# Closing feed-forward stage: where the cast and the lower half of a weight part stand in the engines' queues

## The chip, the cores and the metric

The kernel runs on one core of a Trainium2 chip. The metric is the device time of one execution in microseconds (us), the median of three runs. Engines: PE is TensorE (PEld its weight loads), DVE is VectorE, ACT is ScalarE, POOL is GpSimd, SP is SyncE, which issues the DMAs spoken of here.

## The reference

Three layers follow one another: an attention layer (2 batches, 8 heads, 576 positions, head width 64, rotary positions), a layer of 8 experts with top-1 routing over the 1152 tokens, and a dense feed-forward layer. Only the last one is touched:

```python
def _moe2_ref(x, w_in, w_out, alpha):      # x 1152x512, w_in 512x2048, w_out 2048x512
    h = x @ w_in
    g = np.maximum(h, 0.0) + alpha * np.minimum(h, 0.0)
    return (g @ w_out).astype(np.float32)
```

The rows of `x` that no expert kept are zero, and the kernel sorts the kept tokens into columns, so that the closing stage runs over 784 columns with these inputs.

## The kernel before, in words

Every product is made of three passes (`PASS`): each float32 operand is split into an upper half, a cast to fp32r, and a lower half, what is left; the passes are upper x upper, upper x lower, lower x upper. The weights of the closing layer come from memory as 64-bit numbers.

The closing stage is `ffn`, called by `short_way` with the blocks (272, 256, 256) and the tag "a". The hidden width of 2048 is 16 steps `f`, and four steps are a quarter `mg`. `up(f)` makes three blocks, one for each range of columns: twelve matmuls on PE into one of four PSUM banks (L1124), two Relu of that bank on ACT (L1133, L1134), a sum of them on DVE (L1136, called the blend here), a cast on ACT (L1141) and the lower half on POOL (L1142). The cast and the lower half of a block are put into the list `later` and enter the queues at the next `flush()`, which stands behind the two Relu of the next block. `down(mg)` makes six tiles of 128 columns, twelve matmuls each (L1188), summed by DVE (L1198, L1200) out of three PSUM banks in turn. Behind the first of the six tiles stands `down_strip` (L1157), eight narrow matmuls for the 16 columns left over, which need a copy by POOL (L1146) from the last block of each step `f`. The order is up(0) to up(4), down(0), up(5) to up(8), down(1), up(9) to up(12), down(2), up(13) to up(15), down(3). So three times a run of up blocks ends in a first tile.

A weight group `g` has four parts: group 2*mg is the quarter of w_in that up uses, group 2*mg+1 the quarter of w_out that down uses. `split2` turns one part (128 x 512) into its two halves: three DVE instructions at once (L1020 to L1022, bit operations that make a float32 of a 64-bit number), and `rest`, returned for later: a cast on ACT (L1025) and a subtraction on POOL (L1026, the lower half of the part). The buffer `raw2` that a group lies in is loaded again by `load2`, a DMA on SP, once its last part is split.

`pace()` is called at the end of each block and each tile and counts them in `slots[0]`: slots 1 to 15 are up blocks, 16 to 21 tiles, 22 to 33 blocks, 34 to 39 tiles, 40 to 51 blocks, 52 to 57 tiles, 58 to 66 blocks, 67 to 72 tiles. `piece()` starts one part: group 1 at the ends of slots 7, 8, 9, 10, group 4 at 14, 16, 18, 20, group 3 at 22, 24, 26, 28, group 6 at 32, 34, 36, 38, group 5 at 40, 42, 44, 46, group 7 at 48, 50, 52, 54. `need(g)` stands ahead of the first use of a group and flushes: group 1 ahead of slot 16, 4 ahead of 31, 3 ahead of 34, 6 ahead of 49, 5 ahead of 52, 7 ahead of 67.

The program order is each engine's order: the schedule is written by hand, and every engine takes its own instructions in that order.

Of the kernel before, what the change touches and what calls it, by code (L numbers as in the profile page):

```python
# [845 lines left out]
def build(nc, tc, cap, q, k, v, wg, w1, w2, w_in, w_out, alpha, tab, rtab, out):  # L846
    assert 0 < cap <= W
    with ExitStack() as top:
# [149 lines left out]
        with ExitStack() as ctx:  # L998
# [12 lines left out]
            def w2_hl(g):  # L1011
                return hl[(3, 0, 2, 1)[g % 4]]

            def split2(src, ht, c):


                hw, lw = src[:, :, 1], src[:, :, 0]
                t = cv[:, next(turns)]
                v = nc.vector
                v.tensor_scalar(t, hw, 3, 0x3FFFFFFF, op0=ALU.logical_shift_left, op1=ALU.bitwise_and)  # L1020
                v.scalar_tensor_tensor(hw, hw, 0xC0000000, t, op0=ALU.bitwise_and, op1=ALU.bitwise_or)
                v.scalar_tensor_tensor(hw, lw, 29, hw, op0=ALU.logical_shift_right, op1=ALU.bitwise_or)  # L1022

                def rest():
                    nc.scalar.copy(ht[:, 0, c], hw.bitcast(F32))  # L1025
                    nc.gpsimd.tensor_tensor(ht[:, 1, c], hw.bitcast(F32), ht[:, 0, c].bitcast(F32), op=ALU.subtract)  # L1026

                return rest

            def rows64(dst, src):  # L1030
                nc.sync.dma_start(
                    dst.rearrange("p c f w -> p c (f w)"), src.bitcast(U32).rearrange("(c p) f -> p c f", p=P)
                )
# [3 lines left out]
            def src2(c):  # L1037
                mg = c // 2
                if c % 2 == 0:
                    return w_in[:, mg * 512 : mg * 512 + 512]  # L1040
                return w_out[mg * 512 : mg * 512 + 512, :]

            def make_ffn(zp, gp, tp, pf, po, pt):
# [11 lines left out]
                def ffn(c0, blocks, tag, first, early=()):  # L1055
# [6 lines left out]
                        side = pt(f"side_{tag}")  # L1062
                        nc.vector.memset(gs, 0.0)

                    done, later = [0, 0], []

                    def flush():
                        while later:
                            later.pop(0)()

                    seq = ([0, 2] if first else []) + [1, 4, 3, 6, 5, 7]
                    raw_of = lambda g: raw2[seq.index(g) % 2]
                    src_of = lambda g, c: rawy[:, c] if g == 1 and c < 2 and not first else raw_of(g)[:, c]
                    pieces = [(g, c) for g in seq for c in range(4)]

                    def load2(i):
                        if i < len(seq):
                            g = seq[i]
                            half = g == 1 and not first
                            rows64(raw_of(g)[:, 2 if half else 0 : 4], src2(g)[256 if half else 0 : 512])  # L1080
# [5 lines left out]
                    def piece(n=1):  # L1086

                        for _ in range(n):
                            if not pieces or pieces[0][0] // 2 - 1 > done[pieces[0][0] % 2]:
                                return  # L1090
                            g, c = pieces.pop(0)
                            later.append(split2(src_of(g, c), w2_hl(g), c))
                            if c == 3 and not (strip and g % 2):
                                later.append(lambda: load2(seq.index(g) + 2))

                    slots = [0]

                    def pace():


                        slots[0] += 1
                        if (slots[0] > LEAD or first) and (slots[0] % 2 == 0 or slots[0] <= 2 * LEAD and not first):
                            piece()

                    def need(g):

                        while any(p[0] == g for p in pieces):
                            n = len(pieces)
                            piece()
                            assert len(pieces) < n  # L1110
                            flush()
                        flush()

                    def up(f):
                        if f % 4 == 0:
                            need(f // 4 * 2)
                        wt = w2_hl(f // 4 * 2)
                        g = gt[f % NG]
                        for bi, (lo, hi) in enumerate(zip(edges, edges[1:])):
# [13 lines left out]
                            nc.scalar.activation(A, ps, AF.Relu)  # L1133
                            nc.scalar.activation(Bn, ps, AF.Relu, scale=-1.0)  # L1134
                            flush()
                            nc.vector.scalar_tensor_tensor(A, Bn, nal[:, f : f + 1], A, op0=ALU.mult, op1=ALU.add)  # L1136

# [40 lines left out]
                    def down(mg):  # L1178
                        need(2 * mg + 1)
                        wt = w2_hl(2 * mg + 1)  # L1180
                        for t, m in tiles:
                            if strip and t == 1:
                                down_strip(mg)
                            ps = po(f"d_{tag}_{mg}_{t}")
                            for c in range(4):
                                g = gt[(4 * mg + c) % NG]
                                for i, (a, b) in enumerate(PASS):
                                    nc.tensor.matmul(  # L1188
                                        ps[:m],
                                        lhsT=g_cols(g, b, t * P, t * P + m),  # L1190
                                        rhs=wt[:, a, c, :],
                                        start=(c == 0 and i == 0),
                                        stop=(c == 3 and i == 2),
                                    )
                            flush()
                            sc = wgt[:m, t, 0:1]
                            if mg == 0:
                                nc.vector.tensor_scalar(acc2(t, m), ps[:m], sc, None, op0=ALU.mult)  # L1198
                            else:
                                nc.vector.scalar_tensor_tensor(  # L1200
                                    acc2(t, m), ps[:m], sc, acc2(t, m), op0=ALU.mult, op1=ALU.add
                                )
                            pace()
                            if mg == 3:
                                finish(t, m, acc2(t, m))
                                if strip and t == 3:
                                    finish_strip()
# [423 lines left out]
```

## Time and profile before

| | |
|---|---|
| median of 3 runs | 464.43 us (464.12 to 465.53) |
| the profiled execution | 468.51 us, of which the span from the first to the last instruction is 466.7 us |
| closing stage in that span | from 302 us to 460 us |
| mean granted TensorE clock over the span | 0.982 |

Times within a trace are counted from the start of the span. The idle time in brackets in a timeline is that of the engine just ahead of the instruction, with what ended it.

### The profile page before, as it was taken

Reading aid. Unit: us, or ns where it says so; the run is one execution under the profiler, and the core shown is the slowest. Engines: PE = TensorE matmul, PEld = TensorE weight load, DVE = VectorE, ACT = ScalarE, POOL = GpSimd, SP = SyncE. Lnnn points to the kernel's source line nnn. Section 1 sums busy time; section 2 is a strip of 40 time slices with the busy share of each in tenths; the row PEclk is TensorE's granted clock in tenths of the full one; section 3 lists DMA queues with packets and bytes.
Section 4 is the critical chain, followed back from the end, with each engine's and each line's share of the span. In section 5 each row is a group of like instructions: output and inputs, shape, how many; then the busy total and the mean of one; then the engine's idle time right before and its main releaser. Section 6 shows DMA issues by size and latency. Waiting matters only on the chain. (4 is left out here: it accounts for less than half of the span.)

```text
span 466.7 us, 8223 instructions
## 1 busy us (share of the span) xinstructions
PE 421.9 (90%) x2993; PEld 332.2 (71%) x2993; DVE 305.5 (65%) x563; ACT 216.1 (46%) x540; POOL 238.7 (51%) x280
## 2 busy tenths in 40 slices
PE   6789999999989999995878798998999899889993
PEld 3576666666666666695867798697689589758962
DVE  8996566574777464579489911139888797886321
ACT  2476767666665667342253331164424514432600
POOL 6578482864775334148645310047736745662532
PEclk9999999999999999999899898999999999999998
DMA  7422999604031624467466667940314045000012
GB/s 215 129 60 48 175 332 295 185 1 121 0 119 35 195 88 160 158 228 250 104 208 216 235 222 264 374 170 1 122 60 180 5 178 183 0 1 0 2 69 73
DMA packets 37329, 63.71 MB, mean 137 GB/s; under 512 B 9886, under 2 KB 16158, under 8 KB 37280
## 3 DMA queue, kind: packets, MB, share of 16 engines
q1 hardware_dynamic: 35424, 58.83, 39.7%
q0 software_dynamic: 1568, 3.95, 2.3%
q8 instruction: 25, 0.41, 0.4%
q10 hardware_dynamic: 288, 0.33, 0.2%
q14 instruction: 24, 0.20, 0.1%
HBM read 47.35 MB, written 11.65 MB: 126 GB/s over the span
## 5 line engine op out<-in xcount | busy, mean ns | idle before, releaser
L308 DVE TENSOR_REDUCE nm<-S 128x1 f32<-128x576 f32 x72 | 54.2, 755 | 45.0 <-PE S L299 27.7
L309 ACT ACTIVATE P<-S,nm 128x576 f32<-128x576 f32 x72 | 53.5, 742 | 52.6 <-DVE nm L308 51.0
L1124 PE MATMUL u_a<-yh,whl 128*128 128x256 f32 (+1 forms) x576 | 71.3, 284 | 6.1 <-ACT room L1134 5.7
L1124 PEld LDWEIGHTS u_a<-yh,whl 128*128 128x128 f32 x576 | 70.1, 188 | 7.4 <-ACT room L1134 6.4
L1136 DVE SCALAR_TENSOR_TENSOR room<-room,nal 128x256 f32<-128x256 f32 (+1 forms) x48 | 30.5, 637 | 30.9 <-ACT room L1134 30.8
L330 PEld LDWEIGHTS pt<-ident,P 128*128 128x128 f32 x256 | 27.0, 141 | 29.3 <-ACT P L309 6.8
L1026 POOL TENSOR_TENSOR whl<-wraw,whl 128x512 fp32r<-128x512 f32 x22 | 28.9, 1312 | 35.8 <-ACT whl L1025 32.7
L363 PE MATMUL av<-PT,v 128*64 128x288 f32 x256 | 44.7, 431 | 0.4 <-DVE PT L319 0.3
L1188 PE MATMUL acc<-whl,split_room 128*128 128x512 f32 x162 | 42.3, 396 | 2.2 <-DVE xs L1200 1.2
L330 PE MATMUL pt<-ident,P 128*128 128x128 f32 x256 | 41.5, 286 | 3.1 <-ACT P L309 2.9
L1025 ACT CAST whl<-wraw 128x512 fp32r<-128x512 f32 x22 | 14.5, 657 | 54.2 <-DVE wraw L1022 54.2
L1188 PEld LDWEIGHTS acc<-whl,split_room 128*128 128x128 f32 x162 | 29.7, 188 | 13.1 <-DVE xs L1200 2.9
L1142 POOL TENSOR_TENSOR g<-room,g 128x272 fp32r<-128x272 f32 (+2 forms) x21 | 17.7, 853 | 41.7 <-ACT g L1141 39.2
L299 PE MATMUL S<-T,T 128*128 128x288 f32 x112 | 36.1, 338 | 1.1 <-DVE T L178 1.1
L1188 PE MATMUL acc<-whl,g 128*128 128x512 f32 x126 | 32.9, 391 | 0.5 <-POOL whl L1026 0.5
L299 PE MATMUL S<-X,T 128*128 128x288 f32 x112 | 31.2, 293 | 0.0
L154 POOL TENSOR_TENSOR hl<-R,hl 128x512 fp32r<-128x512 f32 x12 | 15.4, 1287 | 30.6 <-ACT hl L153 30.5
L1142 POOL TENSOR_TENSOR split_room<-room,split_room 128x272 fp32r<-128x272 f32 (+2 forms) x27 | 24.6, 919 | 12.3 <-ACT split_room L1141 9.5
L1188 PEld LDWEIGHTS acc<-whl,g 128*128 128x128 f32 x126 | 23.5, 188 | 6.6 <-POOL whl L1026 0.9
L319 DVE COPY PT<-pt 128x512 f32<-128x512 f32 (+1 forms) x32 | 19.9, 623 | 12.2 <-PE pt L330 7.9
L319 ACT COPY PT<-pt 128x512 f32<-128x512 f32 (+1 forms) x48 | 26.0, 544 | 3.6 <-PE pt L330 3.4
L927 POOL TENSOR_TENSOR whl<-wraw,whl 128x512 fp32r<-128x512 f32 x12 | 15.9, 1329 | 22.3 <-ACT whl L924 22.3
(290 smaller groups left out, 925.4 us busy)
## 6 DMA issues: line engine op xcount, KB each, us to landing
wraw<-moe_w SPq DMA_DIRECT2D x16, 1024.0 KB, 6.3
wraw<-moe_w_out SPq DMA_DIRECT2D x3, 2048.0 KB, 8.1
x_disp<-zero SPq DMA_DIRECT2D x9, 576.0 KB, 8.0
wraw<-moe_w_in SPq DMA_DIRECT2D x2, 2048.0 KB, 10.1
X<-T SPq DMA_DIRECT2D x14, 288.0 KB, 4.1
room<-moe_w SPq DMA_DIRECT2D x3, 1024.0 KB, 6.5
out<-zero SPq DMA_DIRECT2D x4, 576.0 KB, 7.9
v<-v SPq DMA_DIRECT2D x8, 256.0 KB, 5.2
```

The source lines that it names most:

```text
L299: nc.tensor.matmul(ps[:, half, 0:288], lhsT=lhsT, rhs=rhs, start=(n == 0), stop=(n == len(terms) - 1),)
L308: nc.vector.tensor_reduce(nm, ps[:, :, 0:288], op=ALU.max, axis=AX.XY, negate=True)
L309: nc.scalar.activation(Pt.rearrange("p (a n) -> p a n", a=2), ps[:, :, 0:288], AF.Exp, bias=nm, scale=1.0, accum_out=st["ssum"][:, t, hh : ...
L319: (nc.vector.tensor_copy if SCH["e"][k] else nc.scalar.copy)(o, i)
L330: nc.tensor.transpose(ps[:, kb, :], Pt[:, at : at + 128], ident)
L363: nc.tensor.matmul(ps[64 * hh : 64 * hh + 64, 0:288], lhsT=lhs, rhs=(PT[:, hh, kb] if kb < 4 else PR)[:, half * 288 : half * 288 + 288], s ...
L927: eng.tensor_tensor(ht[:, 1, c], rt[:, c], ht[:, 0, c].bitcast(F32), op=ALU.subtract)
L1026: nc.gpsimd.tensor_tensor(ht[:, 1, c], hw.bitcast(F32), ht[:, 0, c].bitcast(F32), op=ALU.subtract)
L1124: nc.tensor.matmul(ps, lhsT=wt[:, a, c, (f % 4) * 128 : (f % 4) * 128 + 128], rhs=yh_[0][:, b, c, c0 + lo : c0 + hi], start=(c == 0 and i ...
L1136: nc.vector.scalar_tensor_tensor(A, Bn, nal[:, f : f + 1], A, op0=ALU.mult, op1=ALU.add)
L1142: nc.gpsimd.tensor_tensor(g_cols(g, 1, lo, mid), A[:, 0 : mid - lo], hi_.bitcast(F32), op=ALU.subtract)
L1188: nc.tensor.matmul(ps[:m], lhsT=g_cols(g, b, t * P, t * P + m), rhs=wt[:, a, c, :], start=(c == 0 and i == 0), stop=(c == 3 and i == 2),)
```

## The change

A part's cast and lower half, and the load that follows a group's last part, go into a list of their own, `parts`, with the slot at which the part was started and its group. `flush(group)` first empties `later`, then takes from the head of `parts` what belongs to the group asked for, or what was started at a slot at least two below the count. The three DVE instructions stay where they are.

```diff
-                    done, later = [0, 0], []
+                    done, later, parts = [0, 0], [], []
-                    def flush():
+                    def flush(group=None):
                         while later:
                             later.pop(0)()
+                        while parts and (parts[0][1] == group or parts[0][0] + 2 <= slots[0]):
+                            parts.pop(0)[2]()
...
                             g, c = pieces.pop(0)
-                            later.append(split2(src_of(g, c), w2_hl(g), c))
+                            parts.append((slots[0], g, split2(src_of(g, c), w2_hl(g), c)))
                             if c == 3 and not (strip and g % 2):
-                                later.append(lambda: load2(seq.index(g) + 2))
+                                parts.append((slots[0], g, lambda: load2(seq.index(g) + 2)))
...
                             n = len(pieces)
                             piece()
                             assert len(pieces) < n
-                            flush()
-                        flush()
+                            flush(g)
+                        flush(g)
```

## Rows read from the trace of the kernel before

**Rows 1.** Busy time by engine in four stretches: length, PE, PEld, DVE, ACT, POOL, clock, DMA
```profile
302.00:333.00 31.00, 27.72 (x201) 24.38 (x201) 20.65 (x30) 16.22 (x49) 18.67 (x21) 1.00 0.22 83
346.00:373.00 27.00, 24.44 (x172) 21.11 (x171) 20.85 (x29) 14.10 (x40) 17.18 (x19) 1.00 0.21 79
385.00:413.00 28.00, 25.02 (x175) 21.58 (x174) 21.58 (x28) 13.45 (x37) 17.14 (x18) 1.00 0.22 77
413.00:427.00 14.00, 12.78 (x56) 9.93 (x55) 12.77 (x17) 3.54 (x9) 7.51 (x8) 1.00 0.00 0
```

**Rows 2.** Who waited for whom from 310 us on: total us, times, longest us
```profile
ACT whl L1025 <- DVE wraw L1022: 54.2, 22, 3.3
...
PE u_a L1124 <- ACT room L1134: 5.7, 3, 2.3
...
PE acc L1188 <- DVE xs L1200: 1.2, 2, 0.8
```

**Rows 3.** Timeline of PE, closing stage: start, us, instruction, idle before
```profile
325.32 1.69 PE L1124 MATMUL u_a<-yh,whl 128*128 128x256 f32 x12 [2.33 <-ACT room L1134]
...
332.92 1.65 PE L1188 MATMUL acc<-whl,g 128*128 128x512 f32 x6
...
346.65 14.65 PE L1124 MATMUL u_a<-yh,whl 128*128 128x272 f32 x120
...
369.11 0.50 PE L1188 MATMUL acc<-whl,split_room 128*128 128x512 f32 x1 [0.48 <-POOL whl L1026]
...
372.03 0.98 PE L1188 MATMUL acc<-whl,split_room 128*128 128x512 f32 x3
...
442.95 1.26 PE L1157 MATMUL acc<-wraw,room 128*32 128x512 f32 x8
444.14 2.34 PE L1188 MATMUL acc<-whl,split_room 128*128 128x512 f32 x9
```

**Rows 4.** Timeline of all engines, end of the second run of blocks
```profile
361.01 0.69 DVE L1022 SCALAR_TENSOR_TENSOR wraw<-wraw 128x512 uint32<-128x512 uint32 x1
361.62 0.48 DVE L1136 SCALAR_TENSOR_TENSOR room<-room,nal 128x256 f32<-128x256 f32 x1
361.74 0.65 ACT L1025 CAST whl<-wraw 128x512 fp32r<-128x512 f32 x1 [2.38 <-DVE wraw L1022]
...
362.47 1.30 POOL L1026 TENSOR_TENSOR whl<-wraw,whl 128x512 fp32r<-128x512 f32 x1 [2.04 <-ACT whl L1025]
...
368.34 1.00 DVE L1136 SCALAR_TENSOR_TENSOR room<-room,nal 128x256 f32<-128x256 f32 x1 [0.96 <-ACT room L1134]
...
370.55 0.41 POOL L1146 COPY room<-room 128x16 f32<-128x16 f32 x1
...
371.34 0.42 DVE L1020 TENSOR_SCALAR cv<-wraw 128x512 uint32<-128x512 uint32 x1
```

**Rows 5.** Timeline of all engines, first run of blocks
```profile
317.56 0.69 DVE L1021 SCALAR_TENSOR_TENSOR rawy<-rawy,cv 128x512 uint32<-128x512 uint32 x1
317.58 1.84 POOL L1026 TENSOR_TENSOR whl<-rawy,whl 128x512 fp32r<-128x512 f32 x1 [1.34 <-ACT whl L1025]
...
327.74 0.47 DVE L1136 SCALAR_TENSOR_TENSOR room<-room,nal 128x256 f32<-128x256 f32 x1
...
328.66 1.30 POOL L1026 TENSOR_TENSOR whl<-wraw,whl 128x512 fp32r<-128x512 f32 x1 [1.38 <-ACT whl L1025]
...
331.44 0.41 POOL L1146 COPY room<-room 128x16 f32<-128x16 f32 x1
```

**Rows 6.** Busy time and granted clock in two stretches of the expert layer, as rows 1
```profile
212.00:220.00 8.00, 3.36 (x25) 2.88 (x23) 7.79 (x13) 2.66 (x4) 7.18 (x2) 1.00 1.00 317
220.00:228.00 8.00, 7.86 (x50) 7.84 (x51) 5.44 (x12) 2.14 (x4) 6.07 (x6) 0.79 0.53 151
```

**Rows 7.** Timeline of SP's queue
```profile
349.04 0.37 SPq L1031 DMA_DIRECT2D wraw<-moe_w_in  x1
```

**Rows 8.** The page's DMA issues: count, KB each, median us to landing
```profile
wraw<-moe_w_in SPq DMA_DIRECT2D x2, 2048.0 KB, 10.1
```

## Prediction

> **What bounds the kernel now.** Read the busy time of the closing stage first [rows 1]: PE works 27.72 of 31 us, 24.44 of 27, 25.02 of 28 and 12.78 of 14. So PE sets the pace, and all that anything here can win is its idle time: 3.28 + 2.56 + 2.98 + 1.22 = 10.0 us. The list of waits says what PE waits for [rows 2]: 5.7 us in three waits for the second Relu to free a PSUM bank, and 1.2 us for DVE's sums to free a down bank. The rest sits in the first tile of each quarter. The same list has the reason for the three long ones: ACT stands 54.2 us, 22 times, in front of a part's cast until DVE's last step for that part is done, and the Relu that would free the bank are queued behind that cast.
>
> Then read the timeline across one seam, the second [rows 3, 4]. The blocks run from 346.65, 120 matmuls (ten blocks) in 14.65 us, 1.465 a block. In the first tile the twelfth matmul waits for POOL's lower half of a part (0.48 us, at 369.11); then the strip waits for POOL's copy, which ends at 370.55 + 0.41 = 370.96; PE goes on with the second tile at 372.03. From there it does not wait until the next run of blocks. So each stage is one question: when does PE get past its first tile and strip? That time I call the join.
>
> What sets it is not DVE alone. The two rows of the first run [rows 5] show a POOL subtraction of 1.84 us that began while a DVE step of 0.69 us had just begun; the same subtraction alone takes 1.30 [rows 4]. It lost 0.54 us, most of that step. DVE and POOL take turns here, and between the blocks one of the two is nearly always at work: DVE 20.85 and POOL 17.18 of 27 us [rows 1], waits for turns included.
>
> **What the change does, counted.** A part started at the end of slot s is now flushed in block s+1. After the change the flush of block s+1 sees the count s, that of s+2 sees s+1, and only that of s+3 sees s+2. So by the code it is two blocks later, not one, and three at most from the start. The exceptions are the parts of slots 10, 28 and 46, which the flushes of `need` ahead of slots 13, 31 and 49 take. No instruction is added or removed; 24 casts, 24 lower halves and two loads (behind groups 4 and 6) move. In the tiles ACT has nothing else queued, so there the move costs nothing: the cast still runs when DVE is done, since what stands ahead of it is done too. With that cover gone (a Relu ahead) it is a seam, treated below.
>
> *The loads.* The load behind group 4 is issued at 349.04 now [rows 7], behind the lower half of slot 20, which moves behind block 23, some 4 us on; it lands in about 10.1 us [rows 8], by 363, and DVE first reads that buffer at 371.34 [rows 4]. Eight us of slack hide it; on SP nothing is queued behind it that is due earlier. The other such load lies alike.
>
> *ACT.* The Relu no longer stand behind the wait for DVE, so the three waits of 5.7 us shrink or go. But PE then only comes to its first tile sooner. The last part's lower half is what it needs there, and that is the one moved back: the cast of slot 28 entered the queue ahead of the Relu of block 30, and now stands behind the cast of block 30, which needs that block's blend. Its lower half now stands behind POOL's copy for the strip.
>
> *Second stage.* The blend of block 30 ends at 368.34 + 1.00 = 369.34 now [rows 4], and the strip's copy 1.62 later. After the change the last lower half (1.30) comes behind that copy; its cast (0.65, behind a smaller one) fits in the 1.62. So PE is released 1.62 + 1.30 = 2.92 behind the blend. How much earlier does the blend come? Below: DVE and POOL both pause between 361.62 + 0.48 = 362.10 and 362.47, 0.37 us, because the lower half waits for its cast; three such pauses in the run, 1.1 us, go. Above: DVE's own waits for the Relu, 0.96 at this blend [rows 4], three of them, 2.9 us, if POOL's work in those gaps cost DVE nothing. (The lower half of slot 20 enters the run and that of slot 28 leaves it ahead of the blend, so the work is equal.) I take 1.4, near the lower end, because POOL's 1.30 at 362.47 fills most of such a gap and DVE would have met it. Release: 369.34 - 1.4 + 2.92 = 370.86. Then the twelfth matmul, 0.50, and eight strip matmuls without a wait, 444.14 - 442.95 = 1.19 [rows 3]: the join is 372.55 against 372.03, +0.5; the bounds give +0.8 and -1.0.
>
> On that choice the Trainium skill's page "SBUF — State Buffer", section "Who interferes with whom", has a rule: VectorE and GpSimd share a port pair under an exclusive lock, which a VectorE instruction with two SBUF inputs takes too. By it only pauses of both count, 1.1 us, and the stage would be +0.8; by DVE's waits alone it would be -1.0. The 1.84 against 1.30 agrees with the page.
>
> *First stage.* Four parts come in four blocks, so no part is added to the run. The strip's copy ends at 331.44 + 0.41 = 331.85 now [rows 5], with all four lower halves ahead of it. The common pause from 327.74 + 0.47 = 328.21 to 328.66, 0.45, goes; the last lower half falls behind the copy, and the two blends of blocks 13 and 14 (0.48 each [rows 4]) can slip ahead of it: 331.85 - 0.45 + 0.96 = 332.36, join 334.05 against 332.92 [rows 3], +1.1. Bounds: no blend ahead +0.2, the pause not regained +1.6.
>
> *Third stage.* As the second, +0.5, but here a part is started at slot 48, so three DVE steps (0.42, 0.69, 0.69 [rows 4, 5]) compete with the last copy and lower half: between 0 and 1.8, and I take one lost turn, 0.54 [rows 5]. Against that, the cast of slot 48 no longer holds the Relu of blocks 49 to 51, DVE reaches its sums earlier, and the 1.22 us behind this seam [rows 1, 2] go: +0.5 + 0.5 - 1.2 = -0.2; bounds -2.2 and +1.4.
>
> The last run of blocks has no parts in it; group 7 is late by a tile at most and is needed after 440. Nothing there.
>
> *The clock.* PE would reach its first tile of stage one at 325.32 - 2.33 + 1.47 = 324.46 [rows 3] and be released at 332.36: 7.9 us with eleven matmuls in it, about 2.7, so 5.2 idle. In the second stage it is 346.65 + 12 x 1.465 = 364.2 to 370.86, 6.6 us, 3.9 idle. Now these waits are spread and the clock is 1.00 throughout [rows 1]. The nearest row elsewhere: PE busy 3.36 of 8 us, 4.64 idle, and the next 8 us ran at 0.79 [rows 6]. With two levels, 2.4 and 1.2 GHz, 0.79 is 0.42 x 8 = 3.4 us at the lower one, 1.7 us lost. I charge that once, to stage one, whose 5.2 idle exceed that row's 4.64; zero and three times are the ends. The skill's page "TensorE: Matmul & The Clock Gate", section "HAM oscillation — how this bites in real kernels", tells of a kernel in which waits between groups of matmuls bring the lower rate back each time. By it the charge would be three times 1.7, and the sum +6.5.
>
> **The sum.** 1.1 + 0.5 - 0.2 + 1.7 = +3.1 us. The profiled execution of 468.51 would be 471.6, its span 469.8. That execution lies 4.1 us above the median; the change is the same on both, so the median becomes 467.5.
>
> **Rivals.**
> *A: the two orders cancel.* Clock stays at 1.00, and in stage one no blend slips ahead: +0.2 + 0.5 - 0.2 = +0.5, 464.9. For it: 2.33 us of waiting in one go did not lower the clock now [rows 1, 3]. Against: the waits become one lump.
> *B: the clock falls behind all three first tiles.* 1.4 + 3 x 1.7 = +6.5, 470.9. For it: the 3.9 us of waits in stage two come near the 4.64 of rows 6. Against: they stay under them.
> *C: faster, the chain of blends was held by ACT.* If DVE's waits of 0.96 really are its own, the blends come 2.9 earlier, and the release overtakes today's: +0.2 - 1.0 - 2.2 = -3.0, 461.4. It decides from 1.9 us of earlier blend on, where stage two turns negative. Against it are the turns that DVE and POOL take [rows 5].
> That it does something else than it says (two blocks, not one) is read from the code and already in the numbers.
>
> **How the numbers follow.** Forecast (one or two falls, +1.4 to +5) 0.42; A 0.25; B 0.15; C 0.18. The likeliest gives 467.5, by itself 465.9 to 469.5. The range takes in A and the middle of B, and leaves out most of C: 463.0 to 471.0. What a measurement of this kernel can tell from no change is about 0.3%, 1.4 us: faster than that 0.18, within 0.25, slower 0.57.
>
> **What would show it.** Right: the wait of ACT in front of L1025 falls from 54 us to a few; PE's waits for the Relu go; the twelfth matmul of the first tiles waits several times 0.5 us, on L1026 or the cast, and no wait for the strip's copy is left; the joins move by +1.1 and +0.5 before any change of clock; the 1.2 us on DVE's sums go; a slice of the clock under 1.00 lies behind 330. Wrong: the join of the second stage comes earlier than 372 relative to its first block (C), or the clock stays whole (A), or the loads land too late and DVE waits in front of L1020.

## Result and the profile after

The changed kernel takes 469.2 us (median of 12 runs, 466.83 to 470.56) against 464.35 us (12 runs, 461.94 to 466.31) of the kernel before on the same chip: ratio 1.0102, 95% interval 1.0078 to 1.0125. It is slower by 4.85 us; the forecast was slower by 3.1. Of 63 executions of the kernel before in the experiments, two, of 567.96 and 773.93 us, are outliers and are left out.

Its profiled execution took 467.68 us with a span of 466.0, less than the profiled one of before. That does not contradict the medians: the closing stage begins at 296.42 us there and at 302.07 before, though nothing ahead of it was changed, and over all the profiles in this study it begins between 296.4 and 303.5. So the closing stage is measured by itself, from the start of its first matmul to the end of its last. These are its last matmuls, before and after:

```profile
458.39 0.84 PE L1188 MATMUL acc<-whl,g 128*128 128x512 f32 x3
...
457.64 0.84 PE L1191 MATMUL acc<-whl,g 128*128 128x512 f32 x3
```

Before: 458.39 + 0.84 - 302.07 = 157.16 us. After: 457.64 + 0.84 - 296.42 = 162.06 us. The difference, 4.90, is close to that of the medians, 4.85.

These are the busy times of the closing stage cut at the first matmul of each run of blocks; the first three pieces are stages one to three, the kernel before first (length, then PE, PEld, DVE, ACT, POOL busy, granted clock, DMA share, GB/s):

```profile
302.07:346.65 44.58, 41.37 (x260) 35.68 (x261) 33.67 (x46) 18.56 (x52) 25.50 (x27) 1.00 0.29 104
346.65:385.80 39.15, 36.59 (x225) 31.11 (x224) 32.32 (x43) 16.37 (x44) 23.10 (x24) 1.00 0.29 108
385.80:427.13 41.33, 37.13 (x225) 30.95 (x224) 33.59 (x43) 16.98 (x45) 24.66 (x25) 1.00 0.15 52
427.13:459.20 32.07, 32.07 (x191) 26.57 (x189) 9.66 (x16) 9.36 (x28) 12.96 (x18) 1.00 0.10 36
```

And the same four of the changed kernel:

```profile
296.42:344.32 47.90, 44.45 (x261) 37.06 (x261) 33.09 (x46) 18.60 (x52) 24.49 (x27) 0.89 0.26 96
344.32:383.52 39.20, 35.90 (x225) 30.91 (x224) 34.95 (x43) 16.29 (x44) 23.18 (x24) 1.00 0.29 108
383.52:426.39 42.87, 38.35 (x225) 32.05 (x224) 36.35 (x43) 16.98 (x45) 26.03 (x25) 0.92 0.14 50
426.39:458.48 32.09, 32.09 (x191) 26.57 (x189) 9.66 (x16) 9.34 (x28) 12.94 (x18) 1.00 0.10 37
```

Stage one is 3.32 us longer, stage three 1.54, stage two and the rest within 0.1. The two longer stages are those in which the clock is not 1.00. In them PE is also busier, 44.45 against 41.37 and 38.35 against 37.13 us for the same matmuls: its idle time grew by 0.24 and 0.32 us only, the rest is that it worked more slowly.

The list of waits of the changed kernel (us in total, times, longest), which answers to [rows 2]:

```profile
ACT whl L1025 <- DVE wraw L1022: 20.4, 6, 4.7
...
PE acc L1191 <- POOL whl L1026: 5.7, 5, 2.4
...
PE acc L1191 <- ACT whl L1025: 3.7, 3, 1.4
...
PE u_a L1127 <- ACT room L1137: 1.8, 2, 0.9
```

and two more lines of the list of the kernel before:

```profile
PE acc L1157 <- POOL room L1146: 1.5, 3, 0.8
PE acc L1188 <- POOL whl L1026: 1.5, 3, 0.5
```

Of ACT's 54.2 us in front of the casts 20.4 are left, six times. PE's waits for the Relu went from 5.7 to 1.8 us, and those for the strip's copy (1.5 us before) and for DVE's sums are gone. In their place PE waits 9.4 us for lower halves and casts of weight parts, against 1.5 before. The timeline of PE shows where, with the lines that answer to [rows 3]:

```profile
320.59 0.50 PE L1191 MATMUL acc<-whl,g 128*128 128x512 f32 x1 [0.87 <-POOL whl L1026]
322.52 1.22 PE L1191 MATMUL acc<-whl,split_room 128*128 128x512 f32 x2 [1.43 <-ACT whl L1025]
324.04 1.65 PE L1191 MATMUL acc<-whl,split_room 128*128 128x512 f32 x3 [0.29 <-POOL whl L1026]
326.54 0.79 PE L1191 MATMUL acc<-whl,split_room 128*128 128x512 f32 x1 [0.85 <-POOL whl L1026]
...
329.12 2.93 PE L1191 MATMUL acc<-whl,g 128*128 128x512 f32 x6
331.85 1.73 PE L1191 MATMUL acc<-whl,split_room 128*128 128x512 f32 x6
333.42 1.54 PE L1191 MATMUL acc<-whl,g 128*128 128x512 f32 x6
...
344.32 16.07 PE L1127 MATMUL u_a<-yh,whl 128*128 128x272 f32 x132
361.29 1.69 PE L1127 MATMUL u_a<-yh,whl 128*128 128x256 f32 x12 [0.90 <-ACT room L1137]
...
366.34 0.74 PE L1191 MATMUL acc<-whl,split_room 128*128 128x512 f32 x2 [1.16 <-ACT whl L1025]
368.32 0.50 PE L1191 MATMUL acc<-whl,split_room 128*128 128x512 f32 x1 [1.25 <-POOL whl L1026]
...
369.79 0.96 PE L1191 MATMUL acc<-whl,split_room 128*128 128x512 f32 x3
...
405.56 0.73 PE L1191 MATMUL acc<-whl,g 128*128 128x512 f32 x2 [1.16 <-ACT whl L1025]
408.73 0.80 PE L1191 MATMUL acc<-whl,g 128*128 128x512 f32 x1 [2.44 <-POOL whl L1026]
...
411.32 2.93 PE L1191 MATMUL acc<-whl,split_room 128*128 128x512 f32 x6
```

Look at the durations, not only at the waits. Six matmuls of a tile take 1.52 to 1.54 us once PE runs; at 329.12 and at 411.32 they take 2.93. The twelfth matmul of the first tile, 0.50 us in stage two, takes 0.79 and 0.80 in stages one and three. The clock by itself, in stretches around the two seams:

```profile
318.00:327.00 9.00, 5.55 (x17) 2.98 (x16) 6.83 (x9) 4.53 (x14) 7.54 (x8) 0.72 0.00 1
327.00:333.00 6.00, 6.00 (x20) 3.29 (x20) 5.90 (x7) 0.96 (x2) 3.81 (x5) 0.56 0.38 120
363.00:370.00 7.00, 4.60 (x21) 2.18 (x21) 5.37 (x7) 3.74 (x11) 5.18 (x6) 1.00 0.00 1
402.00:409.00 7.00, 3.40 (x14) 2.12 (x12) 6.93 (x9) 3.55 (x12) 6.14 (x7) 0.88 0.00 0
409.00:415.00 6.00, 6.00 (x19) 3.20 (x20) 5.90 (x7) 1.93 (x4) 4.55 (x6) 0.57 0.01 3
```

The price of a fall: from the release of the twelfth matmul to the next run of blocks, stage one takes 344.32 - 326.54 = 17.78 us and stage three 426.39 - 408.73 = 17.66. Stage two, at a full clock, takes 383.52 - 368.32 = 15.20. So the falls of the clock cost about 2.6 and 2.5 us here.

### The profile page after: what moved, and what is told of

It reads as the page before. It is cut to its first block, busy times and chain, and to the rows that moved or that the text cites. A ratio compares the mean times of both kernels' runs of the same rounds, so it can differ in the third digit from the quotient of the medians.

```text
span 466.0 us, 8215 instructions
## 1 busy us (share of the span) xinstructions
PE 422.4 (91%) x2993; PEld 332.8 (71%) x2993; DVE 313.1 (67%) x563; ACT 216.3 (46%) x540; POOL 239.7 (51%) x280
## 5 line engine op out<-in xcount | busy, mean ns | idle before, releaser
L308 DVE TENSOR_REDUCE nm<-S 128x1 f32<-128x576 f32 x72 | 54.2, 754 | 46.6 <-PE S L299 31.3
L1191 PE MATMUL acc<-whl,split_room 128*128 128x512 f32 x162 | 45.5, 416 | 5.0 <-ACT whl L1025 2.6
L1139 DVE SCALAR_TENSOR_TENSOR room<-room,nal 128x256 f32<-128x256 f32 (+1 forms) x48 | 32.4, 694 | 23.9 <-ACT room L1137 23.9
L1191 PEld LDWEIGHTS acc<-whl,split_room 128*128 128x128 f32 x162 | 31.4, 199 | 17.8 <-POOL whl L1026 4.3
L1026 POOL TENSOR_TENSOR whl<-wraw,whl 128x512 fp32r<-128x512 f32 x22 | 31.8, 1446 | 15.3 <-ACT whl L1025 13.2
L1191 PE MATMUL acc<-whl,g 128*128 128x512 f32 x126 | 35.4, 410 | 4.5 <-POOL whl L1026 3.3
L1145 POOL TENSOR_TENSOR split_room<-room,split_room 128x272 fp32r<-128x272 f32 (+2 forms) x27 | 23.1, 862 | 27.4 <-ACT split_room L1144 20.9
L1191 PEld LDWEIGHTS acc<-whl,g 128*128 128x128 f32 x126 | 24.5, 197 | 12.8 <-POOL whl L1026 4.8
L1136 ACT ACTIVATE room<-u_a 128x256 f32<-128x256 f32 (+1 forms) x48 | 18.6, 387 | 29.6 <-PE u_a L1127 29.4
L154 POOL TENSOR_TENSOR hl<-R,hl 128x512 fp32r<-128x512 f32 x12 | 15.4, 1286 | 32.1 <-ACT hl L153 32.1
L927 POOL TENSOR_TENSOR whl<-wraw,whl 128x512 fp32r<-128x512 f32 x12 | 15.7, 1309 | 18.0 <-ACT whl L924 18.0
```

The lines of the kernel that those rows point to most:

```text
L308: nc.vector.tensor_reduce(nm, ps[:, :, 0:288], op=ALU.max, axis=AX.XY, negate=True)
L1145: nc.gpsimd.tensor_tensor(g_cols(g, 1, lo, mid), A[:, 0 : mid - lo], hi_.bitcast(F32), op=ALU.subtract)
L1191: nc.tensor.matmul(ps[:m], lhsT=g_cols(g, b, t * P, t * P + m), rhs=wt[:, a, c, :], start=(c == 0 and i == 0), stop=(c == 3 and i == 2),)
```

## Experiments

The measure in all of them is the closing stage, cut at the joins (the first matmul of the second tile) and at the next first block. "To join" counts from the first block of a stage, "on" from the join to the next run of blocks; the clock is that of the three stages. The last run, 32.1 us, never changed.

The closing stage is read from one profiled execution of each kernel, the ratio from its 6 to 12 timed executions against those of the kernel before on the same chip. Of the experiments e1 to e4 ran on one chip and e5 to e8 on another; there the kernel before takes 467.74 us (35 executions) and 463.89 (26). Some expectations name medians, meant against 464.4. On the slower chip they came as 468.64 (e1), 469.53 (e2), 466.40 (e3) and 466.41 us (e4), so that the ratio has to answer for them. Every difference of the closing stage lies inside the interval of its ratio.

| kernel | closing stage | stage 1 to join, on | stage 2 | stage 3 | clock | ratio of times (95%) |
|---|---|---|---|---|---|---|
| before | 157.16 | 30.85, 13.73 | 25.38, 13.77 | 25.79, 15.54 | 1.00 1.00 1.00 | |
| changed | 162.06 | 32.70, 15.20 | 25.47, 13.73 | 27.80, 15.07 | 0.89 1.00 0.92 | 1.0102 (1.0078 to 1.0125) |
| e1, one block | 158.19 | 31.75, 14.09 | 26.23, 14.41 | 25.83, 13.78 | 0.96 0.96 1.00 | 1.0042 (1.0010 to 1.0074) |
| e2, filled in 1 and 3 | 160.12 | 31.66, 13.73 | 26.87, 15.33 | 26.69, 13.74 | 1.00 0.92 1.00 | 1.0062 (1.0028 to 1.0096) |
| e3, only group 7 late | 156.54 | 30.86, 13.77 | 25.34, 13.73 | 25.79, 14.95 | 1.00 1.00 1.00 | 0.9982 (0.9952 to 1.0012) |
| e4, last part of w_out prompt | 154.66 | 30.26, 13.74 | 24.74, 13.73 | 25.15, 14.94 | 1.00 1.00 1.00 | 0.9969 (0.9936 to 1.0002) |
| e5, filled in all three | 157.47 | 31.61, 13.73 | 25.79, 13.74 | 26.71, 13.74 | 1.00 1.00 1.00 | 1.0012 (0.9979 to 1.0045) |
| e6, only three parts late | 161.34 | 30.96, 13.74 | 27.52, 14.06 | 27.64, 15.32 | 1.00 0.96 0.92 | 1.0115 (1.0073 to 1.0157) |
| e7, only groups 4 and 6 late | 159.03 | 30.85, 13.74 | 26.31, 13.74 | 26.75, 15.55 | 1.00 0.96 1.00 | 1.0069 (1.0037 to 1.0101) |
| e8, every last part prompt | 152.26 | 30.26, 13.74 | 23.52, 13.74 | 23.95, 14.95 | 1.00 1.00 1.00 | 0.9907 (0.9874 to 0.9939) |

The diffs are against the changed kernel.

**The clock or the lateness: e2 and e5.**

```diff
-                            ps = po(f"d_{tag}_{mg}_{t}")
+                            ps = ahead.pop() if ahead else po(f"d_{tag}_{mg}_{t}")
+                            if t == 0 and FILL.get(mg):
+                                ahead.append(po(f"d_{tag}_{mg}_{t}_next"))
...
+                                    for _ in range(FILL.get(mg, {}).get((c, i), 0) if t == 0 else 0):
+                                        nc.tensor.matmul(ahead[0], lhsT=yh_[0][:, 0, 0, 0:128],
+                                            rhs=yh_[0][:, 0, 0, 0:512], start=True, stop=True)
```

e2 has `FILL = {0: {(1, 2): 4, (2, 0): 7, (3, 2): 4}, 2: {(3, 0): 5, (3, 2): 11}}`, e5 also `1: {(3, 0): 5, (3, 2): 7}`.

> The changed kernel with extra matmuls that PE runs where it would wait in the first tiles of stage one (4 + 7 + 4 of them) and stage three (5 + 11), about 0.23 us each, into the next tile's bank, which that tile overwrites. The result is the same. Theory (the loss is the clock): the granted clock stays at 1.00 in both stages, the releases stay where they are in the changed kernel (30.1 us after the stage's first matmul, 25.1 us after the first block of stage three), and the closing stage takes 157 to 158 us instead of 162.1; the median is 464 to 465.5. Rival (the late release is the loss, the clock only its shadow): the joins and the time stay, 468 to 470, or more with the extra work.

Stages one and three came as the clock theory said: 1.00, the releases (the start of the twelfth matmul) where they were, 30.19 and 25.22 us behind the first block, and on from the join in 13.73 and 13.74. But stage two, left alone, now lost the clock (0.92, 15.33 on from the join), with nearly the waits that had left it whole in the changed kernel's profile (0.91, 1.15 and 1.54 us against 0.90, 1.16 and 1.25). Its twelfth matmul:

```profile
368.32 0.79 PE L1201 MATMUL acc<-whl,split_room 128*128 128x512 f32 x1 [1.54 <-POOL whl L1026]
```

The total was missed for that reason, and the run said nothing yet on the sum. Hence e5:

> The changed kernel with extra matmuls in all three first tiles (stage one 4 + 7 + 4, stage two 5 + 7, stage three 5 + 11), into the next tile's bank, which that tile overwrites. With fill in stages one and three alone, the clock held there and fell in stage two. Theory (the loss is the clock): 1.00 in all three stages, closing stage 157 to 157.8 us, equal to the 157.2 before, though every release stays late. Rival (late release): 160 or more, at a full clock.

The three stages of e5, by the same cut:

```profile
296.42:341.76 45.34, 43.92 (x275) 38.01 (x276) 33.66 (x46) 18.59 (x52) 24.57 (x27) 1.00 0.28 105
341.76:381.29 39.53, 38.61 (x238) 33.08 (x236) 34.93 (x43) 16.43 (x44) 23.44 (x24) 1.00 0.30 107
381.29:421.74 40.45, 39.53 (x241) 33.84 (x240) 36.62 (x43) 16.99 (x45) 26.10 (x25) 1.00 0.15 53
```

and two lines of its PE timeline at the third seam, the filler and the twelfth matmul behind it, which does not wait any more:

```profile
403.90 2.69 PE L1197 MATMUL acc<-yh 128*128 128x512 f32 x11
406.53 0.51 PE L1201 MATMUL acc<-whl,g 128*128 128x512 f32 x1
```

The casts and lower halves stand in the queues as late as in the changed kernel; PE only rests less in the first tiles (0.80 and 0.62 us in that of stage one, none in the other two). That alone brings the closing stage from 162.06 to 157.47, 0.31 us above before, and the time to no measurable difference. So 4.6 of the 4.9 us are the clock. The other 0.3 need not be the order of the queues: in stage two the release is 24.00 us behind the first block in the changed kernel and 24.32 in e5, because the last lower half, 1.30 us there, took longer here, as it did in e2 without filler in that stage (1.57 us, release 24.28):

```profile
364.43 1.60 POOL L1026 TENSOR_TENSOR whl<-wraw,whl 128x512 fp32r<-128x512 f32 x1
```

**Which late parts: e6, e3, e7.** Each changes the condition in `flush` so that only some parts wait (tuples carry the part's number `c` as a fourth entry where it is used).

```diff
-                        while parts and (parts[0][1] == group or parts[0][0] + 2 <= slots[0]):
e6:
+                        while parts and (parts[0][1] == group or parts[0][1] == 7 or parts[0][1] % 2 == 0
+                                         or parts[0][3] < 3 or parts[0][0] + 2 <= slots[0]):
e3:
+                        while parts and (parts[0][1] in (group, 1, 4, 3, 6, 5) or parts[0][0] + 2 <= slots[0]):
e7:
+                        while parts and (parts[0][1] in (group, 1, 3, 5, 7) or parts[0][0] + 2 <= slots[0]):
```

> Only the last part of groups 1, 3 and 5 is late (three casts and three lower halves in all); the other 21 are flushed as before. Theory (those three are the late ones that PE waits for): the waits for the Relu stay, 5 us or more, the release moves behind the strip's copy, joins 0.2 to 1 us later than before in each stage, closing stage 158 to 160 us; if the waits are split enough the clock stays at 1.00. Rival (the loss needs all parts to be late): 157.2, as before.

Three late parts of 24 are enough: 161.34 us, 4.2 of the 4.9 us of loss, and 1.3 more than the upper end of what was expected. The joins of stages two and three are 2.14 and 1.85 us later. Their releases, 24.93 and 25.05 us behind the first block, would make that some 1.0 and 0.7 at a full clock (1.47 us from release to join); the rest is the clock, which fell in both. Stage one kept its clock and is 0.11 later, a little under the expected 0.2. The waits for the Relu stay at 5.7 us as expected, and the twelfth matmuls wait besides:

```profile
PE u_a L1127 <- ACT room L1137: 5.7, 3, 2.3
PE acc L1191 <- POOL whl L1026: 5.5, 3, 2.2
```

> Only the parts of group 7 (slots 48 to 54) are late; all others are flushed as before. Theory: the three first tiles stay as before (joins 30.9, 25.4 and about 25.8 us or less), the clock stays at 1.00, and only the two waits for DVE's sums behind the third go, worth 1.2 to 1.8 us: closing stage 155.3 to 156, median 462.6 to 463.2. Rival (a late part costs wherever it is, because DVE and POOL are full): no gain, 464.4 or more.

Stages one to three to the join are those of before, and only the way on from the third join is shorter, 14.95 against 15.54: 0.6 of the 1.2 to 1.8 expected, since one wait for DVE's sums (0.89 us) is left. In the time it is not to be told from no change.

> Only groups 4 and 6 (parts of w_in, not needed in a first tile) are late; in the queues that moves little more than the last part of each, out of the tiles into the next run of blocks. Theory (DVE and POOL take turns in a run, so 1.3 us of POOL work more in it is 1 us or more at the join): stage one as before, stages two and three 0.8 to 1.3 us later, closing stage 158.8 to 160 us at a full clock. Rival (POOL has room in the run): 157.2, as before.

Stage three at a full clock is the clean one: 26.75 against 25.79, +0.96 for one POOL subtraction of 1.3 us, with its cast, moved out of the tiles into a run of blocks. That the subtraction does it, and not the cast on ACT, is seen where DVE falls behind. The lines are of e7 first, then of the kernel before, whose stage begins 1.80 us later in its trace:

```profile
389.36 2.94 POOL L1026 TENSOR_TENSOR whl<-wraw,whl 128x512 fp32r<-128x512 f32 x2
391.06 1.53 DVE L1020 TENSOR_SCALAR cv<-wraw 128x512 uint32<-128x512 uint32 x1
...
392.86 0.97 DVE L1020 TENSOR_SCALAR cv<-wraw 128x512 uint32<-128x512 uint32 x1
```

The DVE instruction starts at the same point, 7.06 us behind the first block, and so does the Relu ahead of it on ACT (5.36 and 5.37); beside the two subtractions it takes 0.56 us longer. The part's third DVE step is slowed likewise (1.08 against 0.70), and the blend behind it ends at 11.27 against 10.29. Stage two came +0.93 with its clock at 0.96; there the fall cost nothing at the join, since PE runs through where it waited before (0.48 and 0.37 us). POOL has no room in these runs: most of what is put in comes out at the join.

**How late: e1.**

```diff
-parts[0][0] + 2 <= slots[0]
+parts[0][0] + 1 <= slots[0]
```

> Every part one block earlier than in the changed kernel, so truly one block later than before. Theory (the changed kernel loses almost only by the granted clock, which falls because PE's waits in a first tile become one lump before the last lower half): the last lower half enters POOL's queue ahead of the last block's own lower half and the strip's copy, the lump shrinks, the clock stays at 1.00 in all three first tiles, and the closing stage (from its first matmul to its last) takes 155 to 157.5 us against 157.2 before and 162.1 in the changed kernel; the median is 462.5 to 464.5. Rival (any part that leaves ACT free of the wait for DVE makes the release late, and the lateness itself is the loss): 467 or more, joins later by 1 us or more at a full clock.

The total lies where neither theory put it, at 158.19: the theory missed by 0.7 us, and its clock did not hold (0.96 in stages one and two). In stage one the waits of the first tile are 1.28, 1.43 and 0.78 us, in sum 3.49 against 3.44 in the changed kernel, so one block less does not break up the lump there. In stage three the clock held, and the join came level with before.

**Only the last part prompt: e4 and e8.** e4 looks at a fourth entry that is true for the last part of an odd group, e8 at that of any group:

```diff
-                        while parts and (parts[0][1] == group or parts[0][0] + 2 <= slots[0]):
e4:
+                        while parts and (parts[0][1] == group or any(p[3] for p in parts) or parts[0][0] + 2 <= slots[0]):
e8:
+                        while parts and (parts[0][1] == group or any(p[3] == 3 for p in parts) or parts[0][0] + 2 <= slots[0]):
```

> As the changed kernel, but once the last part of a w_out group (1, 3, 5, 7) has been started, all parts in the list go at the next flush, as before the change; the parts ahead of it stay late. Theory (what hurts is the last lower half alone): the joins come no later than before, the clock stays at 1.00, the waits for DVE's sums go: closing stage 154.5 to 157, median 461.5 to 464.4. Rival (late casts hurt one and all): 467 or more, with a slice of the clock below 1.00 in stage one.

> The first three parts of every group late, the last part of every group at the next flush as before the change. Against the run in which only w_out's last parts were prompt (closing stage 154.7), the last parts of groups 4 and 6 go back into the tiles. Theory: stages two and three come another 0.8 to 1.3 us earlier each, closing stage 152.3 to 153.2 us, clock 1.00, 0.9% or more faster than before. Rival (no gain from it): 154.7.

e4 holds the clock, and every join is earlier than before, by 0.59, 0.64 and 0.64. One wait for DVE's sums, of 0.85 us, is left against the expectation, and by its time e4 is not told from no change. e8 takes the last parts of groups 4 and 6 out of the runs again, and stages two and three gain another 1.22 and 1.20, what one such subtraction (1.3 us) weighs. e8 is faster than both kernels: 152.26 us for the closing stage, 4.9 less than before, and a time ratio of 0.9907 (459.61 us). Its second seam answers to the lines of [rows 3, 4]; 341.66 is its first block, and the DVE line holds the blends of blocks 29 and 30:

```profile
341.66 17.50 PE L1127 MATMUL u_a<-yh,whl 128*128 128x272 f32 x144
...
359.52 2.98 DVE L1139 SCALAR_TENSOR_TENSOR room<-room,nal 128x256 f32<-128x256 f32 x2
...
362.27 0.50 PE L1191 MATMUL acc<-whl,split_room 128*128 128x512 f32 x1 [0.48 <-POOL whl L1026]
...
363.70 0.41 POOL L1149 COPY room<-room 128x16 f32<-128x16 f32 x1
```

The blend of block 30 ends at 362.50, 20.84 us behind the first block against 22.69 before, and the strip's copy at 22.45 against 24.31. Everything is 1.86 us earlier, PE waits the same 0.48 for the same part, and no wait for a Relu is left in that run: all 144 matmuls go through in 17.50 us.

## Why the prediction was right, and where its sizes were off

The sign and the mechanism held, and the measured 469.2 lies within the range. But the sum of 3.1 against 4.85 is made of two terms that were off in opposite ways, and that it came this near is in part luck: with only the first put right it would have been +2.0, with only the second +6.0.

**The order of the queues, forecast +1.4, measured +0.3.** e5 gives it at a full clock: joins +0.76, +0.41 and +0.92 against the forecast +1.1, +0.5 and +1.0 (0.5 + 0.5), and the way on from the third join -1.80 against -1.2. In stage two the changed kernel itself, at a full clock, shows only +0.09. The way on was undersized because the forecast took the matmuls' idle time alone, 1.22 us; the whole way from the join to the next blocks, 15.54 us and then 13.74, shows what those two waits cost. Not all of the 1.80 is due to the late casts of group 7: with the join as before, in e3, the way on is 0.59 shorter, and in e5 PE also comes 0.92 later to sums that DVE finishes earlier. The releases themselves were near: behind the first block of its stage 30.29 forecast and 326.54 - 296.42 = 30.12 measured in the changed kernel, 24.21 and 24.00, 25.1 (the forecast join, 25.79 + 1.0, less 0.50 and 1.19) and 25.21. From the release to the join the forecast took 0.50 + 1.19 = 1.69 us; at a full clock it is 369.79 - 368.32 = 1.47.

**The chain in the second stage** went as worked out. These lines of the changed kernel answer to [rows 4]; the DVE line holds the blends of blocks 29 and 30:

```profile
363.38 1.93 DVE L1139 SCALAR_TENSOR_TENSOR room<-room,nal 128x256 f32<-128x256 f32 x2
...
366.82 0.21 POOL L1149 COPY room<-room 128x16 f32<-128x16 f32 x1
...
366.97 1.30 POOL L1026 TENSOR_TENSOR whl<-wraw,whl 128x512 fp32r<-128x512 f32 x1
```

The blend ends at 365.31, 20.99 us behind the first block against 22.69: 1.7 earlier, where 1.4 was taken. The last lower half stands right behind the strip's copy and ends at 368.27, 2.96 behind the blend, where 2.92 was worked out. DVE and POOL taking turns, the ground for taking the lower end, is borne out by e7 (+0.96 for 1.3 us of POOL work, and DVE's 1.53 beside it instead of 0.97) and by the 1.2 us a stage between e4 and e8. That agrees with the exclusive port of the Trainium skill's page "SBUF — State Buffer", section "Who interferes with whom".

**The clock, forecast +1.7, measured +4.6.** This is the step that was mis-sized: "I charge that once, to stage one". It fell twice, and each fall cost some 2.5 us where 1.7 had been taken. The row taken for its price, 0.79 over 8 us [rows 6], had 3.4 us at the lower level; in stage one the stretches 318 to 327 at 0.72 and 327 to 333 at 0.56 hold 5.0 + 5.3 us of it (0.28 and 0.44 over one half, times 9 and 6 us), and although part of that is waiting, the strip, the second tile and the start of the third ran at half speed. Stage three, with 3.6 us of waits in its first tile (1.16 + 2.44), had been left out.

**The rivals.** A named the sum of the order, +0.5 forecast and +0.3 measured, but by luck: its +0.2 in stage one was +0.76 and its -0.2 in stage three 0.92 - 1.80 = -0.88; and it had the clock wrong. B came near the clock's sum, 5.1 against 4.6, with three falls of 1.7 us where there were two of 2.5, which is luck as well. The Trainium skill's page "TensorE: Matmul & The Clock Gate", section "HAM oscillation — how this bites in real kernels", stood behind it: waits between groups of matmuls bring the lower rate back. The trace agrees for two of three stages in the changed kernel (0.89 and 0.92), and not for the second (1.00). C was wrong for this change: the blends came 1.7 us earlier, under the 1.9 from which it would decide. Its mechanism is real: with the last part prompt, e8, the blends come 1.85 us earlier and the stage gains it.

**What was to show it.** The twelfth matmuls wait 0.85, 1.25 and 2.44 us on L1026, PE's waits for the strip's copy and for DVE's sums are gone, and slices of the clock lie under 1.00. The waits for the Relu did not go, 1.8 us are left; ACT's wait in front of the casts is 20.4 us, not a few: six casts in the tiles, where nothing is queued behind them that is due. The later loads made nothing wait.

## What to carry to other kernels

Take an instruction that waits for another engine out of the way of what is queued behind it, but look for the one consumer that needs it first: of each group of four parts, three may come late and the fourth may not. The same edit with that exception (e8) wins 0.9%, without it the kernel loses 1%.

A wait of TensorE has two prices, its length and the clock it may cost afterwards; before explaining a loss by the wait itself, look at the duration of the matmuls behind it and at the granted clock of the stage. Filling the wait with matmuls nobody needs tells the two apart.

## What was not expected of the hardware

Nearly the same waits did and did not lower the clock. In the second stage 0.90, 1.16 and 1.25 us of waits left it at 1.00 in the changed kernel, and 0.91, 1.15 and 1.54 us in e2 gave 0.92 over the stage; in the kernel before, one wait of 2.33 us left it at 1.00 [rows 1, 3]. The closest pair is in the one profile of e7, the end of the runs of blocks of stages two and three, behind waits of 0.41 and 1.96 us and of 0.42 and 1.97:

```profile
361.26 4.62 PE L1127 MATMUL u_a<-yh,whl 128*128 128x256 f32 x24 [1.96 <-ACT room L1137]
...
401.31 3.10 PE L1127 MATMUL u_a<-yh,whl 128*128 128x256 f32 x24 [1.97 <-ACT room L1137]
```

The same 24 matmuls take 4.62 us in one stage and 3.10 in the other. What decides between them is left open here. That the falls are the rule in the changed kernel is suggested by its timed executions: the mean clock over the span was 0.954 to 0.966 in all 12, and 0.967 to 0.983 in 61 executions of the kernel before on the two chips of the experiments.
